# The tail of a fused attention and adapter kernel, put in another order over other PSUM banks

## The chip, the cores and the metric

The kernel runs on one core of a Trainium2 chip. Its time is the device time of one execution, in microseconds (us). The core has five engines that run side by side, each taking its own instructions strictly in order: TensorE (PE; its weight loads are shown apart as PEld), VectorE (DVE), ScalarE (ACT), GpSimd (POOL) and SyncE (SP), which here issues transfers (DMA). They wait for each other through semaphores. TensorE writes only to PSUM, which has eight banks; one bank holds 128 x 512 fp32 numbers.

## The reference, cut to what matters

```python
# attention: q (4, 12288, 128), kv (4, 384, 32, 128)
kv_pool = kv.reshape(B, H // 4, 4, W // 4, 4, C).mean(axis=(2, 4))
k = v = kv_pool.reshape(B, -1, C) @ w_sr             # 768 keys for each batch
a = softmax(q @ k.transpose(0, 2, 1) / np.sqrt(C))
x = (a @ v).reshape(B * S, 128)                      # 49152 tokens
# mixture of adapters: 8 experts of rank 16, the two best for each token
logits = x @ w_gate
w = softmax(the two largest logits)
out = x + sum over the two: w * ((x @ A[e]) @ B[e])
```

## The kernel before

**Tiles.** The 49152 tokens are cut into 96 chunks of 512, numbered c = 0 to 95, 24 for each batch. A chunk is four blocks (NS = 4) of 128 tokens. In the code of the tail, n is 95, the last chunk; n-1, n-2 and so on are those ahead of it.

**What one chunk goes through.** `scores` (line 318) multiplies keys and queries on TensorE, two of six key blocks at a time, into a PSUM tile of two banks, and ScalarE takes the exponential of it into the tile `tt` (line 327). `weigh` (329) makes the weighted sums in two halves of 12 products each: the values carry seven differences of gate logits and a column of ones beside the 128 channels, so one product gives x, its logits and the softmax sum. `normalise` (342), on VectorE, takes reciprocals, multiplies, and finds the largest logits with `max`. `gate` (358) computes the gates' arguments on GpSimd, `gate_tanhs` (378) takes their tanh on ScalarE. `turned("x", ...)` transposes x on TensorE, and a copy takes it to SBUF. `gated_hidden` (437) multiplies the transposed x with A and VectorE multiplies with the gates, which have been spread over rows through memory (`send_gates`, `load_gates`). `up` (481) multiplies with B into a PSUM bank. The output is either `add_rows` (497: VectorE adds x while it reads PSUM), or `take` (489: ScalarE copies PSUM to SBUF) and then `add` (494: GpSimd adds x, since it works on SBUF here), or `x_first` (474: TensorE puts x into the bank with an fp32 identity ahead of `up`) and `take`. `put` (503) sends 256 KB to memory.

**The last six chunks** have no time for the way through memory: their hidden rows are made token by token (`down`, 451, or `hidden`, 803), VectorE multiplies with the gates (`apply_gate`, 463, or `gated`, 778), and TensorE transposes the product (`turn`, 786, or `turned("h", ...)`), which ScalarE copies to SBUF before `up`.

**The order** of all this is written out by hand (`tc.manual_schedule()`): an instruction stands on its engine's queue where the program names it. The waits between engines are put in when the program is built, from which tile each instruction reads and writes; a PSUM tile of two banks counts as one tile there.

**The main loop** (683) runs c from 2 to 94 and weighs chunk c - 1 in pass c. Its last pass, c = 94 = n-1, has extra steps for n-5 and n-4 (695, 718, 740, 744).

**The tail** (749 to 906) gives up the four banks of the scores and makes of them the tiles `e0`, `e1` and `y5`. It weighs n-1 into the banks of `xps` (`y4`) and n into `y5`, with the outputs of n-7 to n-4 between, and finishes the last chunk in two halves: ScalarE writes one, VectorE the other (901 to 905), and the last `put` goes out on ScalarE's queue. `tail_ok` and `all_ok` (570 to 580) count whether the softmax sums were in range; if not, a slow exact path runs, which these inputs do not need.

**Bank names in the tail.** `t_bank()` is the one bank of the transposes, `mtile` the one bank "hd" of the hidden rows and outputs, `fbank(0)` and `fbank(1)` are made from the two banks of `xps` once these are free.

Of the kernel before, what the change touches and what calls it, by code (L numbers as in the profile page):

```python
# [10 lines left out]
FP32 = mybir.dt.float32  # L11
# [5 lines left out]
ALU = mybir.AluOpType  # L17
# [4 lines left out]
def kernel(  # L22
# [175 lines left out]
    def stile(name):  # L198
        return ps_s.tile([P, 2, NTOK], FP32, tag="sg", name=name)
# [251 lines left out]
    def down(c, bank=None):  # L451
        hps[c] = mtile([P, NS, P], name="h_ps") if bank is None else as_tokens(bank)
        for s in range(NS):
            mm(hps[c][:, s], xT[c][:, s], a_bf, start=(s == 0), stop=(s == NS - 1))
# [48 lines left out]
    def put(c, osb, lo=0, hi=NS, queue=None):  # L503
        t0 = c * NTOK
        (queue or nc.sync).dma_start(
            out[t0:t0 + NTOK, :].rearrange("(p s) c -> p s c", p=P)[:, lo:hi], osb[:, lo:hi])
# [16 lines left out]

    def half_out():
        if not spare:
            o = run.tile([P, 2, NS, P], FP32, tag="osb", name="osb", bufs=3)
            spare.extend([o[:, 0], o[:, 1]])
        return spare.pop(0)

    def chunk_ok(c):  # L530
# [37 lines left out]
            nc.vector.tensor_reduce(tot, cnt, axis=AX.X, op=ALU.add)  # L568

    def tail_ok():  # L570
        nc.gpsimd.tensor_scalar(ok[:, tail], rv[:, tail], 1.0 / L_HI, None, op0=ALU.is_ge)
        nc.gpsimd.tensor_scalar(low, rv[:, tail], 1.0 / L_LO, None, op0=ALU.is_le)

    def all_ok(bank):
        n = (NCH - CUT) * NS
        mm(bank[0:1, 0:n], ones_c, ok[:, tail], start=True, stop=False)
        mm(bank[0:1, 0:n], ones_c, low, start=False, stop=True)
        nc.vector.tensor_reduce(last, bank[0:1, 0:n], axis=AX.X, op=ALU.add)
        full = float(P * (NCH * NS + n) + P * 2 * B + 2 * B)
        nc.vector.tensor_scalar(bad, last, tot, full, op0=ALU.add, op1=ALU.not_equal)  # L580

# [98 lines left out]
    for p in range(OWN // 2):  # L680
        sent[2 * p + 3 + (lag(2 * p + 1) > 8)] = p
        fetched[2 * p + 3 + {9: 3 + (lag(2 * p + 3) > 8), 8: 2, 7: 2, 6: 1}[lag(2 * p + 1)]] = p
    for c in range(2, NCH - 1):
        b, k = divmod(c, CPB)
        if c in fetched and lag(2 * fetched[c] + 1) > 8:
            load_gates(fetched[c])
# [31 lines left out]
        if c == NCH - 2:  # L718
            _, evacuate_h = turned("h", c - 4, stile("t_ps")[:, 0])
        next_scores()  # L720
        prep(c)
        k0 = 19 if b == 0 else 17
# [14 lines left out]
            gated_hidden(x)  # L737
        if c in sent:
            send_gates(sent[c])
        if c == NCH - 2:  # L740
            down(c - 3, stile("h_ps")[:, 0])
            apply_gate(c - 3)
        evacuate(c == NCH - 2)
        if c == NCH - 2:
            evacuate_h(True)

    score_banks.close()
    end_banks = ExitStack()  # L750
    ps_e = end_banks.enter_context(tc.tile_pool(
        name="ps_e", bufs=1, reuse_waits="tile", space=bass.MemoryType.PSUM))

    def bank(i):
        return ps_e.tile([P, NTOK], FP32, tag=f"e{i}", name=f"e{i}")

    def gate_args(c, lo, hi, eng, top, arg, msk):
        lg = xn[c][:, lo:hi, C:C + E]
# [59 lines left out]
    def tops4(c, top, y):  # L818
        ri = rinv_all[:, c]
        xv = y[:, :, 0:2 * VW].rearrange("p b (s v) -> p b s v", v=VW)  # L820
        nc.vector.reciprocal(ri.rearrange("p (b s) -> p b s", b=2), xv[:, :, :, VW - 1])
        nc.vector.tensor_tensor(
            xn[c][:, :, 0:C + G].rearrange("p (b s) v -> p b s v", b=2), xv[:, :, :, 0:C + G],
            ri.rearrange("p (b s) -> p b s", b=2).unsqueeze(3).broadcast_to([P, 2, 2, C + G]),
            op=ALU.mult)
        for s in range(NS):
            nc.vector.max(top[:, s], xn[c][:, s, C:C + E])
# [16 lines left out]
    _, evacuate = turned("x", n - 2)
    _, evacuate_h = turned("h", n - 4, bank(0))
    evacuate(True)
    evacuate_h(True)
    up(n - 6, bank(1))
    o6 = take(n - 6)
    h2 = hidden(n - 3, 0, NS, mtile([P, NTOK], name="h2"))  # L850
    up(n - 5, bank(0))
    gate_args(n - 1, 0, NS, nc.gpsimd, top4, arg4, msk4)
    y5 = ps_e.tile([P, 2, 512], FP32, tag="y5", name="y5")
    weigh(n, 0, y5)
    gated(n - 3, 0, NS, gw[q_ - 1][:, 0:NS], h2)
    put(n - 5, add_rows(n - 5))
    add(n - 6, o6, nc.gpsimd)
    put(n - 6, o6)
    turn(high(n - 1), 0, NS, bank(1), xT, n - 1)
    h3 = hidden(n - 2, 0, NS, t_bank())  # L860
    gated(n - 2, 0, NS, gw[q_ - 1][:, NS:2 * NS], h3)
    weigh(n, 1)
    up(n - 4, bank(0))
    gate_tanh(0, NS, arg4)
    o1 = take(n - 4)
    gate_w(0, NS, nc.gpsimd, arg4, msk4)
    tops4(n, top5, y5)
    tail_ok()
    turn(hg[n - 3], 0, NS, mtile([P, NTOK], name="t2"), hgT, n - 3)
    h4 = hidden(n - 1, 0, NS, bank(1))  # L870
    turn(hg[n - 2], 0, NS, t_bank(), hgT, n - 2)
    turn(high(n), 0, NS, bank(0), xT, n)
    gate_args(n, 0, NS, nc.gpsimd, top5, arg5, msk5)
    gate_tanh(0, NS, arg5)
    up(n - 3, mtile([P, NTOK], name="d2"))
    x_first(n - 1, fbank(1), 0, 2)
    gated(n - 1, 0, NS, arg4, h4)
    up(n - 2, fbank(0))
    put(n - 3, add_rows(n - 3))
    put(n - 2, add_rows(n - 2))  # L880
    x3 = ps_e.tile([P, 2, 512], FP32, tag="y5", name="x3")
    h5 = hidden(n, 0, NS, x3[:, 0])
    turn(hg[n - 1], 0, NS, bank(1), hgT, n - 1)
    gate_w(0, NS, nc.gpsimd, arg5, msk5)
    gated(n, 0, NS, arg5, h5)
    x_first(n - 1, fbank(1), 2, 4)
    up(n - 1)
    o4 = take(n - 1)
    put(n - 1, o4)
    add(n - 4, o1, nc.gpsimd)  # L890
    put(n - 4, o1)
    d5 = as_tokens(x3[:, 1])
    for s in range(2):
        mm(d5[:, s], id_f32, xn[n][:, s, 0:C], start=(s == 0), stop=False, skip_group_check=True)
    turn(hg[n], 0, 2, bank(0), hgT, n)
    turn(hg[n], 2, 4, t_bank(), hgT, n, False)
    all_ok(bank(1))
    for s in range(2):
        mm(d5[:, s], hgT[n][:, s], b_bf, start=False, stop=(s == 1), skip_group_check=True)
    o5 = half_out()  # L900
    nc.scalar.activation(o5[:, 0:2], d5[:, 0:2], AF.Copy)
    d6 = as_tokens(mtile([P, NTOK], name="d6"))
    for s in range(2, 4):
        mm(d6[:, s - 2], hgT[n][:, s], b_bf, start=(s == 2), stop=(s == 3), skip_group_check=True)
    nc.vector.tensor_tensor(o5[:, 2:4], d6[:, 0:2], xn[n][:, 2:4, 0:C], op=ALU.add)
# [128 lines left out]
```

## Time and profile before

| what | value |
|---|---|
| median of three runs | 374.78 us (374.4 to 375.65) |
| the profiled execution | 374.92 us |
| its span, first to last instruction | 373.0 us |
| mean granted TensorE clock | 0.999 |
| PE, DVE, ACT, POOL busy | 96%, 80%, 83%, 60% of the span |
| last exponential ends (line 327) | 355.19 us |
| last weighed sum ends (line 338) | 363.42 us |
| last addition ends (line 905) | 369.63 us |

A row of the timeline gives the start in us from the span's beginning, the duration in us, the engine, the line, the operation, the tile written and the tiles read, their sizes and how many instructions were merged into the row; in brackets stands how long the engine had been idle and what released it. A matmul's row reaches to its modelled end; the next matmul starts before that.

### The profile page before, as it was taken

The page shows a single profiled execution, that of the slowest core. Times are in us where ns is not written, and L with a number is a line of the kernel's source. Part 1 is how long each engine was busy: PE and PEld are TensorE (multiplying, and loading weights), DVE is VectorE, ACT ScalarE, POOL GpSimd, SP SyncE. Part 2 cuts the span into 40 slices and gives each one's busy share as a digit, 9 for nine tenths or more (in the row PEclk, how much of TensorE's full clock was granted, in tenths as well). Part 3 has the DMA queues.
Part 4 walks back from the last instruction along what each step waited for, and adds up shares of the span by engine and source line. Part 5 has one row for each costly group of instructions (what it writes and reads, how often), then busy time and mean ns, then how long its engine had stood idle before and what let it go on. Part 6 is the DMA issues. An engine that isn't in the chain of part 4 may idle for free.

```text
span 373.0 us, 10593 instructions
## 1 busy us (share of the span) xinstructions
PE 358.1 (96%) x3945; PEld 263.0 (70%) x3945; DVE 300.2 (80%) x953; ACT 308.7 (83%) x390; POOL 223.5 (60%) x374
## 2 busy tenths in 40 slices
PE   4979999999999999999999999999999999999985
PEld 1446767777777777777777777777777777677774
DVE  3684558888788788888888888888888889988995
ACT  1559999898888888989888988988888889888844
POOL 1003799989699987755679887755624424323244
PEclk9999999999999999999999999999999999999999
DMA  8997999999999999999999999999879899745424
GB/s 260 386 382 177 286 354 291 281 312 330 323 292 311 317 307 258 286 301 317 312 301 338 339 295 313 251 319 246 247 212 253 245 235 241 215 123 132 156 106 181
DMA packets 95594, 101.01 MB, mean 271 GB/s; under 512 B 58804, under 2 KB 59060, under 8 KB 95540
## 3 DMA queue, kind: packets, MB, share of 16 engines
q1 hardware_dynamic: 93924, 99.85, 94.7%
q8 instruction: 31, 0.51, 0.6%
q10 hardware_dynamic: 1616, 0.46, 0.5%
q14 instruction: 23, 0.19, 0.2%
HBM read 62.33 MB, written 25.90 MB: 237 GB/s over the span
## 4 chain that ended last, share of the span: by engine, by line
PE 84%; DMA 7%; DVE 5%; ACT 1%; issue 1%; SPq 1%; POOL 1%; ACTq 0%; DVEq 0%
PE xps L338 34%; PE sg L326 30%; PE t_ps L405 5%; PE d_ps L486 5%; PE h_ps L440 5%; DMA b_f<-in_moe_B_dram 3%; DMA kvt<-in_kv_dram 2%; DMA ge<-g_h 2%; PE v_ps L215 1%; ACT tt L327 1%; DVE xn_all L349 1%; DVE osb L500 1%; DVE ht L443 1%; SPq L87 1%; PE kp_ps L207 0%
## 5 line engine op out<-in xcount | busy, mean ns | idle before, releaser
L327 ACT ACTIVATE tt<-sg 128x1024 f16<-128x1024 f32 x288 | 276.8, 1022 | 37.2 <-PE sg L326 36.5
L326 PE MATMUL sg<-qT,kfT 128*128 128x512 f16 x576 | 170.2, 379 | 0.4 <-ACT qT L593 0.3
L338 PEld LDWEIGHTS <-tt 128*128 128x128 f16 x2304 | 146.1, 98 | 28.3 <-DVE xn_all L349 18.0
L338 PE MATMUL xps<-vext,tt 128*128 128x136 f16 x2256 | 164.7, 223 | 0.3 <-DVE xn_all L349 0.2
L500 DVE TENSOR_TENSOR osb<-d_ps,xn_all 128x512 f32<-128x512 f32 x85 | 58.7, 691 | 28.6 <-PE d_ps L486 27.6
L365 POOL TENSOR_TENSOR arg<-xn_all,top 128x64 f32<-128x64 f32 x47 | 14.4, 306 | 100.0 <-DVE top L356 80.4
L349 DVE TENSOR_TENSOR xn_all<-xps,rinv_all 128x540 f32<-128x540 f32 x94 | 67.7, 720 | 3.2
L326 PEld LDWEIGHTS <-kfT 128*128 128x128 f16 x576 | 49.1, 98 | 24.4 <-issue 1.5
L191 POOL TENSOR_TENSOR kvt<-kvt 128x1024 f32<-128x1024 f32 x27 | 63.7, 2359 | 2.2 <-PE t_ps L405 2.1
L107 POOL CAST q<-q 128x1024 f16<-128x1024 f32 x45 | 46.8, 1040 | 25.1 <-DMA q<-in_q_dram 25.1
L443 DVE SCALAR_TENSOR_TENSOR ht<-ge,h_ps 128x512 bf16<-128x512 f16 x87 | 58.5, 672 | 1.5 <-DMA ge<-g_h 1.1
L486 PEld LDWEIGHTS <-ht 128*128 128x128 bf16 x368 | 26.9, 98 | 24.8 <-DVE ht L443 6.1
L356 DVE MAX8 top<-xn_all 128x8 f32<-128x8 f32 x376 | 35.1, 156 | 6.3
L416 DVE COPY xt<-t_ps 128x512 bf16<-128x512 bf16 x92 | 36.7, 399 | 0.0
L405 PE MATMUL t_ps<-id_bf,xn_all 128*128 128x128 bf16 x376 | 36.3, 219 | 0.0
L486 PE MATMUL d_ps<-b_bf,ht 128*128 128x128 bf16 x340 | 32.9, 219 | 0.7 <-DVE ht L443 0.7
L440 PE MATMUL h_ps<-xt,a_bf 128*128 128x512 bf16 x87 | 33.0, 379 | 0.1
L345 DVE RECIPROCAL rinv_all<-xps 128x4 f32<-128x4 f32 x94 | 17.1, 182 | 13.7 <-PE xps L338 12.2
L405 PEld LDWEIGHTS <-xn_all 128*128 128x128 bf16 x376 | 25.9, 98 | 0.3
L368 POOL TENSOR_SCALAR msk<-msk 128x64 f32<-128x64 f32 x47 | 20.1, 428 | 4.1
L369 POOL TENSOR_TENSOR arg<-arg,msk 128x64 f32<-128x64 f32 x47 | 15.0, 319 | 3.9
L367 POOL TENSOR_TENSOR arg<-arg,msk 128x64 f32<-128x64 f32 x47 | 15.0, 319 | 3.7
(152 smaller groups left out, 221.0 us busy)
## 6 DMA issues: line engine op xcount, KB each, us to landing
kvt<-in_kv_dram SPq DMA_DIRECT2D x48, 512.0 KB
q<-in_q_dram SPq DMA_DIRECT2D x46, 512.0 KB
out_dram<-osb SPq DMA_DIRECT2D x44, 512.0 KB
ge<-g_h SPq DMA_DIRECT2D x45, 256.0 KB
out_dram<-osb SPq DMA_DIRECT2D x7, 256.0 KB
q<-in_q_dram SPq DMA_DIRECT2D x1, 1024.0 KB
qT<-q SPq DMA_TRANSPOSE x46
g_h<-g_sb SPq DMA_DIRECT2D x45, 16.0 KB
```

Source lines behind the costliest of these rows:

```text
L107: nc.gpsimd.tensor_copy(q16[i], q32[i].rearrange("p k n -> p (k n)"))
L191: eng.tensor_tensor(v[:, 0], v[:, 0], v[:, d], op=ALU.add)
L326: mm(sg[:, k], kfT[b][:, j * P:(j + 1) * P], qc, start=True, stop=True)
L327: nc.scalar.activation(tt[c][:, 2 * r:2 * r + 2], sg, AF.Exp, bias=0.0, scale=scale)
L338: mm(o, tt[c][:, j, s * P:(s + 1) * P], vext[b][:, j, 0:VW], start=(j == 0 and s % 2 == 0), stop=(j == NJ - 1 and s % 2 == 1), skip_group_ ...
L349: nc.vector.tensor_tensor(xn[c][:, :, 0:C + G].rearrange("p (b s) v -> p b s v", b=2), xv[:, :, :, 0:C + G], ri.rearrange("p (b s) -> p b ...
L405: mm(columns(t_ps, c, s), src[:, s], id_bf, is_transpose=True, start=(s == 0), stop=(s == NS - 1), skip_group_check=True)
L416: nc.vector.tensor_copy(to, t_ps)
L440: mm(h_ps, a_bf, xT[c], start=True, stop=True)
L443: nc.vector.scalar_tensor_tensor(hgT[c].rearrange("p (k a) t -> p k (a t)", k=2), gE[c // 2][:, h:h + NS // 2].rearrange("p a t k -> p k ( ...
L486: mm(dps[c][:, s], columns(hgT[c], c, s), b_bf, start=(s == 0 and fresh), stop=(s == NS - 1), skip_group_check=True)
L500: nc.vector.tensor_tensor(osb[:, lo:hi], d, xn[c][:, lo:hi, 0:C], op=ALU.add)
```

## The change

The loop ends one pass earlier, and the tail is written anew:

- The steps of pass n-1 are written out. The score banks are given up after the first half of n-2's weighed sums, and become two tiles of two banks each, `z5` and `z4`. n-1 is weighed into `z4`, n into `z5`; both take later products too: `z4` the output of n-5, the hidden rows of n-3 (its second bank), the outputs of n-4, n-1 and half of n; `z5` the hidden rows of n-5 and n, and the transposes of n-2 and n.
- The outputs of n-8, n-7 and n-5 go from VectorE (`add_rows`) to ScalarE and GpSimd (`take`, `add`). That of n-4 went from ScalarE to GpSimd; now TensorE puts its x into the bank and ScalarE takes it.
- `tops4` multiplies the seven logit columns first, takes the maxima, and multiplies the 128 columns of x last: two multiplications for one.
- The half outputs lie in a tile of the pool `kvpool` instead of `osb` pairs.
- `tail_ok` moves from GpSimd to VectorE; the last comparison (`flag`) goes behind the last addition. `all_ok` stands ahead of the last chunk's transposes, and the last addition of n-6 and n-5 on GpSimd stands behind the gates of n.

```diff
     def half_out():
         if not spare:
-            o = run.tile([P, 2, NS, P], FP32, tag="osb", name="osb", bufs=3)
-            spare.extend([o[:, 0], o[:, 1]])
+            o = kvpool.tile([P, 8, NS, P], FP32, tag="kvt", name="osb")
+            spare.extend(o[:, i] for i in range(8))
...
     def tail_ok():
-        nc.gpsimd.tensor_scalar(ok[:, tail], rv[:, tail], 1.0 / L_HI, None, op0=ALU.is_ge)
-        nc.gpsimd.tensor_scalar(low, rv[:, tail], 1.0 / L_LO, None, op0=ALU.is_le)
+        nc.vector.tensor_scalar(ok[:, tail], rv[:, tail], 1.0 / L_HI, None, op0=ALU.is_ge)
+        nc.vector.tensor_scalar(low, rv[:, tail], 1.0 / L_LO, None, op0=ALU.is_le)
...
-    for c in range(2, NCH - 1):
+    for c in range(2, NCH - 2):
...
+        part(C, C + G)
         for s in range(NS):
             nc.vector.max(top[:, s], xn[c][:, s, C:C + E])
+        part(0, C)
...
+    next_scores()
+    weigh(n - 2, 0)
+    z5 = two("b", "z5")
+    z4 = two("a", "z4")
+    down(n - 5, z5[:, 0])
+    apply_gate(n - 5)
+    up(n - 8)
+    o8 = opair[(n - 8) // 2]
+    nc.scalar.activation(o8[:, 1], dps[n - 8], AF.Copy)
+    add(n - 8, o8[:, 1], nc.gpsimd)
...
+    weigh(n - 2, 1)
+    normalise(n - 2)
+    gate(q_ - 1, nc.gpsimd)
+    turned("x", n - 3)[1](True)
+    weigh(n - 1, 0, z4)
+    turn(hg[n - 5], 0, NS, t_bank(), hgT, n - 5)
+    gated_hidden(n - 7)
+    weigh(n - 1, 1)
+    up(n - 7)
+    o7 = take(n - 7)
+    add(n - 7, o7, nc.gpsimd)
+    put(n - 7, o7)
...
+    down(n - 4, fbank(0))
+    tops4(n - 1, top4, z4)
+    gate_args(n - 1, 0, NS, nc.gpsimd, top4, arg4, msk4)
+    apply_gate(n - 4)
+    gated_hidden(n - 6, fbank(1))
+    turned("x", n - 2)[1](True)
+    gate_tanhs(q_ - 1)
+    weigh(n, 0, z5)
+    up(n - 5, z4[:, 0])
+    o5 = take(n - 5)
+    weigh(n, 1)
+    tops4(n, top5, z5)
+    turn(hg[n - 4], 0, NS, t_bank(), hgT, n - 4)
+    h2 = hidden(n - 3, 0, NS, z4[:, 1])
+    h3 = hidden(n - 2, 0, NS, fbank(0))
+    turn(high(n - 1), 0, NS, fbank(1), xT, n - 1)
+    gate_tanh(0, NS, arg4)
+    gate_w(0, NS, nc.gpsimd, arg4, msk4)
+    gate_args(n, 0, NS, nc.gpsimd, top5, arg5, msk5)
+    up(n - 6)
+    gated(n - 3, 0, NS, gw[q_ - 1][:, 0:NS], h2)
+    gated(n - 2, 0, NS, gw[q_ - 1][:, NS:2 * NS], h3)
+    x_first(n - 4, z4[:, 0], 0, 2)
+    turn(high(n), 0, NS, fbank(1), xT, n)
+    h4 = hidden(n - 1, 0, NS, t_bank())
+    gated(n - 1, 0, NS, arg4, h4)
+    x_first(n - 4, z4[:, 0], 2, 4)
     o6 = take(n - 6)
+    turn(hg[n - 3], 0, NS, mtile([P, NTOK], name="t2"), hgT, n - 3)
+    gate_tanh(0, NS, arg5)
+    gate_w(0, NS, nc.gpsimd, arg5, msk5)
+    up(n - 4)
+    h5 = hidden(n, 0, NS, z5[:, 1])
+    turn(hg[n - 2], 0, NS, z5[:, 0], hgT, n - 2)
+    gated(n, 0, NS, arg5, h5)
     tail_ok()
+    up(n - 3, fbank(0))
+    turn(hg[n - 1], 0, NS, fbank(1), hgT, n - 1)
+    o4 = take(n - 4)
+    put(n - 4, o4)
+    for c, o in ((n - 5, o5), (n - 6, o6)):
+        add(c, o, nc.gpsimd)
+        put(c, o)
+    up(n - 2, t_bank())
     put(n - 3, add_rows(n - 3))
+    x_first(n - 1, z4[:, 1], 0, 4)
+    all_ok(mtile([P, NTOK], name="cnt"))
+    turn(hg[n], 0, 2, z5[:, 0], hgT, n)
+    turn(hg[n], 2, 4, z5[:, 1], hgT, n, False)
     put(n - 2, add_rows(n - 2))
     up(n - 1)
+    o1 = take(n - 1)
+    put(n - 1, o1)
+    d5 = as_tokens(z4[:, 0])
     for s in range(2):
         mm(d5[:, s], id_f32, xn[n][:, s, 0:C], start=(s == 0), stop=False, skip_group_check=True)
     for s in range(2):
         mm(d5[:, s], hgT[n][:, s], b_bf, start=False, stop=(s == 1), skip_group_check=True)
+    o0 = half_out()
+    nc.scalar.activation(o0[:, 0:2], d5[:, 0:2], AF.Copy)
+    d6 = as_tokens(fbank(0))
     for s in range(2, 4):
         mm(d6[:, s - 2], hgT[n][:, s], b_bf, start=(s == 2), stop=(s == 3), skip_group_check=True)
+    nc.vector.tensor_tensor(o0[:, 2:4], d6[:, 0:2], xn[n][:, 2:4, 0:C], op=ALU.add)
+    put(n, o0, queue=nc.scalar)
+    flag()
```

More of the change, by code (lines that the diff above doesn't have):

```diff
@@ L739 @@
             send_gates(sent[c])
[L740 to L755, printed above, removed]
+        evacuate()
     def gate_args(c, lo, hi, eng, top, arg, msk):
@@ L842, in fbank @@
         return ps_f.tile([P, NTOK], FP32, tag=f"f{i}", name=f"f{i}")
[L844 to L848, printed above, removed]
-    o6 = take(n - 6)
[L850 to L867, printed above, removed]
-    tail_ok()
-    turn(hg[n - 3], 0, NS, mtile([P, NTOK], name="t2"), hgT, n - 3)
-    h4 = hidden(n - 1, 0, NS, bank(1))
@@ L882 @@
[L882 to L886, printed above, removed]
-    up(n - 1)
[L888 to L892, printed above, removed]
+    up(n - 1)
+    o1 = take(n - 1)
+    put(n - 1, o1)
+    d5 = as_tokens(z4[:, 0])
     for s in range(2):
         mm(d5[:, s], id_f32, xn[n][:, s, 0:C], start=(s == 0), stop=False, skip_group_check=True)
-    turn(hg[n], 0, 2, bank(0), hgT, n)
```

49 lines of the change are left out of this document (17 added, 32 removed).

## The prediction

> **What bounds the kernel now.** The change touches only the last 20 us, so I read the engines' busy time by stretches there first, and then the timeline. The stretches (PE, PEld, DVE, ACT, POOL busy, then clock, share and GB/s of the transfers):
>
> ```profile
> 350.00:355.00 5.00, 5.00 (x64) 3.91 (x62) 4.41 (x17) 4.75 (x6) 2.01 (x6) 1.00 0.49 159
> 355.00:360.00 5.00, 4.38 (x62) 3.57 (x60) 4.93 (x13) 1.53 (x4) 1.85 (x6) 1.00 0.28 108
> 360.00:365.00 5.00, 4.40 (x72) 3.96 (x70) 4.44 (x15) 3.60 (x8) 3.66 (x11) 1.00 0.36 142
> 365.00:373.00 8.00, 3.81 (x44) 3.08 (x41) 3.43 (x8) 2.89 (x7) 2.62 (x7) 0.95 0.48 178
> ```
>
> Up to 355 TensorE is full. From 355 to 360 VectorE is (4.93 of 5 us) while ScalarE, done with the exponentials, works 1.53 us. After 365 nothing is full: there the tail is a chain of hand-offs from engine to engine. The timeline has its main rows, with the starts that give the prices:
>
> ```profile
> 353.25 1.94 ACT L327 ACTIVATE tt<-sg 128x1024 f16<-128x1024 f32 x2
> 353.70 0.87 PE L338 MATMUL xps<-vext,tt 128*128 128x136 f16 x12
> 354.41 0.39 PE L454 MATMUL h_ps<-a_bf,xt 128*128 128x128 bf16 x4
> 357.95 0.68 DVE L466 TENSOR_TENSOR hgs<-h_ps,th 128x512 bf16<-128x512 f32 x1
> 358.55 0.68 DVE L443 SCALAR_TENSOR_TENSOR ht<-ge,h_ps 128x512 bf16<-128x512 f16 x1
> ...
> 360.10 0.39 PE L486 MATMUL e<-b_bf,ht 128*128 128x128 bf16 x4
> 360.32 0.39 PE L806 MATMUL h<-a_bf,xt 128*128 128x128 bf16 x4
> 360.53 0.59 ACT L414 ACTIVATE ht<-e 128x512 bf16<-128x512 bf16 x1
> 361.17 0.38 PE L486 MATMUL e<-b_bf,ht 128*128 128x128 bf16 x4 [0.47 <-ACT ht L414]
> ...
> 362.36 1.27 POOL L495 TENSOR_TENSOR osb<-osb,xn_all 128x512 f32<-128x512 f32 x1
> 362.55 0.87 PE L338 MATMUL y<-vext,tt 128*128 128x136 f16 x12
> 363.46 0.18 DVE L821 RECIPROCAL rinv_all<-y 128x4 f32<-128x4 f32 x1
> 363.68 0.72 DVE L822 TENSOR_TENSOR xn_all<-y,rinv_all 128x540 f32<-128x540 f32 x1
> 363.69 0.60 ACT L491 ACTIVATE osb<-e 128x512 f32<-128x512 f32 x1 [0.44 <-PE e L486]
> 364.18 0.59 ACT L796 ACTIVATE xr<-t 128x512 bf16<-128x512 bf16 x1
> 364.43 0.37 DVE L827 MAX8 top<-xn_all 128x8 f32<-128x8 f32 x4
> 365.06 0.66 PE L478 MATMUL f<-xn_all,id_f 128*128 128x128 f32 x4
> 365.56 0.39 PE L486 MATMUL f<-b_bf,xr 128*128 128x128 bf16 x4
> ...
> 366.68 0.69 DVE L781 TENSOR_TENSOR hgs<-x,r 128x512 bf16<-128x512 f32 x1
> 367.42 0.71 PE L894 MATMUL x<-xn_all,id_f 128*128 128x128 f32 x4
> 367.97 0.27 PE L790 MATMUL e<-id_bf,hgs 128*128 128x128 bf16 x2
> 368.29 0.27 PE L576 MATMUL e<-ok,ones_c 128*1 128x60 f32 x2
> 368.34 0.38 ACT L796 ACTIVATE xr<-e 128x256 bf16<-128x256 bf16 x1
> 368.39 0.27 PE L577 MATMUL e<-low,ones_c 128*1 128x60 f32 x2
> 369.21 0.42 DVE L905 TENSOR_TENSOR osb<-d,xn_all 128x256 f32<-128x256 f32 x1
> 369.72 0.38 ACTq L505 DMA_DIRECT2D out_dram<-osb  x1
> ```
>
> The last weighed sums end at 362.55 + 0.87 = 363.42, the last addition at 369.63: 6.21 us of chain. Then comes the last transfer, issued at 369.72, and the end at 373.0, 3.3 us on.
>
> **Prices read off these rows.** A group of four 128-wide products occupies TensorE for 0.22 us (360.10 to 360.32) and is there after 0.39. Half a chunk's weighed sums occupy it 0.71 (353.70 to 354.41). Two fp32 products with the identity take 0.50 (365.06 to 365.56), so four take 1.0. A count for `all_ok` takes 0.10 (368.29 to 368.39). On ScalarE a 512-wide copy follows another after 0.48 and is there after 0.60; the half copy takes 0.38. A 512-wide VectorE operation follows after 0.60 and is there after 0.68; the last half addition takes 0.42. GpSimd's addition takes 1.27. A hand-off costs 0.05 (360.53 + 0.59 to 361.17).
>
> **The change, part by part.**
>
> *Weighing earlier.* Both kernels agree up to 354.41. From there TensorE's queue is: hidden rows n-5 0.22, output n-8 0.22, second half n-2 0.71, turn n-3 0.22, first half n-1 0.71, to 356.49. The turn of h n-5 needs the transposes' bank, which ScalarE empties 356.02 to 356.62: a stall to 356.67. Then 0.22 for it and 0.22 for `gated_hidden` n-7, whose product goes to VectorE (357.32 to 358.00); second half n-1 ends sooner, so the output of n-7 waits until 358.05. Four groups (0.88), first half n 0.71, output n-5 0.22, second half n 0.71: the last weighed sums are there at 360.74, 2.68 us earlier than 363.42. The scores' banks cost no wait: `z5` needs the last but one exponential (354.2), `z4`, first used near 355.8, the last (353.25 + 1.94 = 355.19).
>
> *Work moved off VectorE.* Three additions less, 3 x 0.60 = 1.8 us. On ScalarE there are three copies more (1.44 us), on GpSimd two additions more net (2.5), on TensorE the x of n-4 (1.0). These queues are in order: what is queued ahead of the last chunk's steps counts.
>
> *The chain from 360.74.* The built program says which tile each instruction waits for; I walk it with the prices above.
>
> 1. VectorE: hand-off 0.05, reciprocal 0.18, logit product 0.19, maxima 0.36, x product 0.62, two hand-offs in between 0.10, gating of n-3 0.68: 362.92. The new logit product (28 columns) has no row. It lies between the reciprocal's 0.18 and the 0.42 of 256 columns; the slope from 256 to 540 columns (0.42 to 0.72) puts it at 0.19, which I take.
> 2. TensorE has done its five groups behind the weighed sums (5 x 0.22) by 361.7 and has the x of n-4 next, for the first bank of `z4`. VectorE is still reading hidden rows n-3 in the second, and the wait is for the tile. So it idles and starts at 362.97; two fp32 products 0.50, turn of x(n) 0.38, hand-off: ScalarE gets it at 363.90.
> 3. ScalarE: copy of x(n) 0.48, then output n-6 0.60: 364.98. The turn of h(n-3) needs the bank "hd" that output n-6 lies in, and stands at the head of TensorE's queue. 0.05 + 0.38 + 0.05: 365.46.
> 4. ScalarE copies h(n-3): 366.06; 0.05, output n-3 0.22, turn of h(n-1) 0.38, 0.05: 366.77. The tanh of n, ready since 364.1, stood behind that copy; with GpSimd's two steps it lets VectorE gate n at 366.85, against 366.68 before. So logits first buys nothing.
> 5. ScalarE: h(n-1) 0.48, output n-4 from `z4` 0.60: 367.85. The x of n-1 goes into the other bank of `z4` and waits for that: 0.05, four fp32 products 1.0, two counts 0.20, first half turn 0.27, 0.05, and 0.02 for reading waits: 369.44. Ahead of them VectorE's moved range tests have over 1 us of cover; were it gone they would cost at most 2 x 0.42.
> 6. ScalarE copies the half: 369.83. The other half's turn goes into the other bank of `z5` and waits: 0.05 + 0.11, output n-1 0.22 + 0.17, 0.05: 370.43. ScalarE takes output n-1: 371.03.
> 7. The last chunk's x goes into the other bank of `z4` and waits for that: 0.05, two fp32 products 0.50, four products of `up` 0.22 + 0.17, 0.05, last half addition 0.42: 372.44.
>
> The same walk over the kernel before ends at 369.58 (trace 369.63). The difference is **+2.86 us**: 2.68 gained on the way to the last weighed sums, 5.5 lost behind them. What follows moves along: outputs n-2 and n-1 are issued about 1.4 and 1.0 us ahead of the last. SP meets GpSimd's late additions (n-6 ready at 369.3), and n-3 queues behind, but that is over before n-2 (371.1). The comparison put behind the last addition (0.2) lies under the transfer, of which 3.3 us follow. The tile from `kvpool` costs nothing, as the last of the 48 row loads there starts at 222.5:
>
> ```profile
> L87 SPq DMA_DIRECT2D kvt<-in_kv_dram x48: 534/579/1717, 0.7 to 222.5; - x48
> ```
>
> Sum: 374.92 + 2.86 = 377.8 for the profiled execution; that one lies 0.14 above the median of 374.78, so **377.7**.
>
> *Bounds.* With fp32 products at 0.28 each (367.42 to 367.97 for two) and the logit product at 0.42 the difference is 3.45; with hand-offs of 0.03, 2.70; with ScalarE's copies following after 0.44, 2.66; fp32 products at 0.20 would give 2.56. The likeliest case's own range is 377.3 to 378.2 (374.78 + 2.56 and + 3.45).
>
> The clock is granted in full until the core falls quiet:
>
> ```profile
> 372.00:372.20 0.20, 0.00 (x0) 0.00 (x0) 0.00 (x0) 0.00 (x0) 0.00 (x0) 1.00 0.00 0
> 372.20:372.40 0.20, 0.00 (x0) 0.00 (x0) 0.00 (x0) 0.00 (x0) 0.00 (x0) 0.68 0.00 0
> 372.40:373.00 0.60, 0.00 (x0) 0.00 (x0) 0.00 (x0) 0.00 (x0) 0.00 (x0) 0.50 0.00 0
> ```
>
> It falls to half some 3 us after the last products (from 368.90). The new tail has pauses of about 1 us at the most, five of them; I count no loss, and the case that they add up is a rival.
>
> **The rivals.**
>
> *The two banks of a tile do not hold each other up* (no change). Steps 2, 5, 6 and 7 each wait for another bank of the same tile. Without these four waits the walk ends at 369.10, 0.48 before the old one: 374.4. For it: no bank is really shared. Against it: the waits stand in the built program. The Trainium skill, page "PSUM — Partial Sum Buffer", section "PSUM bank collisions raise a hardware error", bears on this: engines collide in one bank, not in different banks, and waits by bank would do. By that rule the four waits are not needed, but the program makes them; no row here shows two engines in two banks of one tile.
>
> *The earlier weighed sums carry to the end* (faster). If ScalarE's queue had no more than before ahead of the last chunk's copies, the old 6.21 us would follow 360.74: 366.95 instead of 369.63, so 372.1. For it: VectorE is the full engine from 355 to 360 and loses 1.8 us. Against it: three added copies and an in-order queue. It decides if gating of n starts before 365 rather than at 366.8.
>
> *Some waits are covered.* Without any single one of the four the walk ends at 371.3 to 371.8, so +1.7 to +2.2: 376.5 to 377.0.
>
> *The clock falls in the pauses.* TensorE's share of the chain from 367.9 on is 1.0 + 0.2 + 0.27 + 0.11 + 0.39 + 0.5 + 0.39 = 2.9 us; at half clock that is 2.9 more: 380.6. Against it: 1.00 in the stretch 360 to 365 with 0.6 us idle. The page "TensorE: Matmul & The Clock Gate", section "The HAM clock gate", of the Trainium skill gives about 3.4 us of idleness before the gate closes; the rows above agree (about 3), and by it this rival doesn't happen.
>
> **How the numbers follow.** Forecast 0.80, some waits covered 0.08, clock 0.02: slower, 0.90. Bank-wise waits 0.04: no change. Carried to the end 0.06: faster. About 0.3% (1.1 us) can be told from no change. "Same" gets 0.04, faster 0.06. The range reaches down over the covered waits, 376.5, and up to the bound of 3.45 us and some tenths for hand-offs that no row shows: 376.4 to 378.9.
>
> **What would show it.** Right: the last weighed sums end near 360.7; then idle TensorE ahead of the fp32 products of n-4, n-1 and n, with ScalarE or VectorE as releaser, about 1 us each; gating of n near 366.85; the last addition near 372.4, and 3.4 us from there to the end. Wrong: weighed sums that end after 362, products of `z4` or `z5` that start while the tile's other bank is being read, or a last transfer that lands over 4 us after its issue.

## The result, and the profile after

| | before | after |
|---|---|---|
| median, five runs each | 374.63 us (374.4 to 375.65) | 377.51 us (376.95 to 378.04) |
| ratio, 95% interval | | 1.0072, 1.0051 to 1.0094 |
| profiled execution, its span | 374.92, 373.0 us | 377.46, 375.7 us |
| mean granted clock | 0.999 | 0.998 |
| hidden rows of n-5 start (line 454) | 354.41 us | 353.78 us |
| last weighed sum ends | 363.42 us | 360.13 us |
| last addition ends | 369.63 us | 372.25 us |

The change made the kernel 2.88 us slower by the medians; 377.7 was predicted. The weighed sums are ready earlier, and the end comes later.

The stretches of the kernel after (columns as before: PE, PEld, DVE, ACT, POOL busy, clock, share and GB/s of the transfers):

```profile
355.00:360.00 5.00, 4.92 (x78) 4.41 (x76) 4.49 (x16) 3.14 (x7) 4.37 (x9) 1.00 0.28 108
360.00:365.00 5.00, 3.57 (x51) 3.21 (x49) 3.22 (x10) 2.70 (x7) 2.63 (x11) 1.00 0.14 52
365.00:370.00 5.00, 3.56 (x39) 2.51 (x36) 3.17 (x5) 2.53 (x6) 2.98 (x4) 1.00 0.39 149
370.00:375.70 5.70, 1.11 (x12) 0.75 (x8) 1.42 (x4) 0.98 (x2) 0.00 (x0) 0.88 0.52 199
```

Up to 360 TensorE is full again, where before it waited for VectorE. From 360 to 365 it is busy 3.57 us where the kernel before had 4.40, and no other engine is full: everyone waits. The clock stays at 1.00 to 370 (and on to 374, well past the last product at 371.8), so the pauses cost no clock.

The timeline of the kernel after, with the rows that answer to those of before (here and in the timelines below, rows in between are left out):

```profile
353.78 0.39 PE L454 MATMUL z<-a_bf,xt 128*128 128x128 bf16 x4
...
359.26 0.87 PE L338 MATMUL z<-vext,tt 128*128 128x136 f16 x12
360.17 0.18 DVE L806 RECIPROCAL rinv_all<-z 128x4 f32<-128x4 f32 x1 [0.18 <-PE z L338]
360.39 0.19 DVE L808 TENSOR_TENSOR xn_all<-z,rinv_all 128x28 f32<-128x28 f32 x1
361.49 0.68 DVE L766 TENSOR_TENSOR hgs<-z,th 128x512 bf16<-128x512 f32 x1
362.23 0.71 PE L478 MATMUL z<-xn_all,id_f 128*128 128x128 f32 x4 [0.98 <-DVE hgs L766]
364.33 0.38 PE L775 MATMUL t<-id_bf,hgs 128*128 128x128 bf16 x4 [0.45 <-ACT osb L491]
366.21 0.69 DVE L766 TENSOR_TENSOR hgs<-z,r 128x512 bf16<-128x512 f32 x1 [2.03 <-POOL r L761]
366.56 0.59 ACT L491 ACTIVATE osb<-z 128x512 f32<-128x512 f32 x1
367.20 1.16 PE L478 MATMUL z<-xn_all,id_f 128*128 128x128 f32 x8 [0.68 <-ACT osb L491]
368.72 0.27 PE L577 MATMUL cnt<-low,ones_c 128*1 128x60 f32 x2 [0.17 <-DVE low L572]
369.24 0.38 ACT L781 ACTIVATE xr<-z 128x256 bf16<-128x256 bf16 x1 [2.10 <-PE z L775]
369.68 0.27 PE L775 MATMUL z<-id_bf,hgs 128*128 128x128 bf16 x2 [0.47 <-ACT xr L781]
370.86 0.71 PE L916 MATMUL z<-xn_all,id_f 128*128 128x128 f32 x4 [0.69 <-ACT osb L491]
371.83 0.42 DVE L924 TENSOR_TENSOR osb<-f,xn_all 128x256 f32<-128x256 f32 x1 [0.89 <-PE f L923]
372.33 0.38 ACTq L505 DMA_DIRECT2D out_dram<-osb  x1
```

The reader is to see the brackets: at 362.23, 367.20, 369.68 and 370.86 TensorE stands idle until another engine has done with the *other* bank of `z4` or `z5` (at 362.23 VectorE's gating of n-3, which began at 361.49 and ends at 362.17). The same from the waits, each engine's idle time put down to who ended it (us in total, times, longest):

```profile
PE z L478 <- DVE hgs L766: 1.0, 1, 1.0
PE z L916 <- ACT osb L491: 0.7, 1, 0.7
PE z L478 <- ACT osb L491: 0.7, 1, 0.7
...
PE z L775 <- ACT xr L781: 0.5, 1, 0.5
PE t L775 <- ACT osb L491: 0.5, 1, 0.5
```

**A measure for the tail.** Both programs are the same up to the hidden rows of n-5 (the first row of line 454), but a single execution reaches that point now earlier, now later: in the profiles of this case it lay between 353.29 and 354.41. Most of that arises near the start of the program: after is 0.24 us later than before at the first exponential, 0.76 earlier at the eleventh (31.4 us in before) and 0.63 earlier at the last. So the experiments are compared by two stretches: from that row's start to the issue of the last chunk's output ("tail"), and from there to the end of the span ("rest"). Before they are 15.31 and 3.3 us, after 18.55 and 3.4. Each tail comes from one profile, but the stretch repeats well: from that row to the end of the last weighed sums it takes 6.34 or 6.35 us in after and in all runs but run 5, which changes it.

### The profile page after: what moved, and what is told of

Read it like the earlier page. It is cut to its first block, busy times and chain, and to the rows that moved or that the text cites. A ratio compares the mean times of both kernels' runs of the same rounds, so it can differ in the third digit from the quotient of the medians.

```text
span 375.7 us, 10604 instructions
## 1 busy us (share of the span) xinstructions
PE 358.6 (95%) x3953; PEld 263.7 (70%) x3953; DVE 300.7 (80%) x954; ACT 310.6 (83%) x393; POOL 225.4 (60%) x374
## 4 chain that ended last, share of the span: by engine, by line
PE 87%; DVE 5%; DMA 4%; ACT 1%; issue 1%; ACTq 0%; SPq 0%; POOL 0%; DVEq 0%
PE xps L338 35%; PE sg L326 31%; PE d_ps L486 6%; PE t_ps L405 6%; PE h_ps L440 5%; DMA b_f<-in_moe_B_dram 3%; DMA kvt<-in_kv_dram 2%; PE v_ps L215 1%; DVE kvt L191 1%; DVE xn_all L349 1%; PE z L338 1%; DVE ht L443 1%; PE kp_ps L207 1%; ACT tt L327 1%; DVE osb L500 0%
## 5 line engine op out<-in xcount | busy, mean ns | idle before, releaser
L338 PEld LDWEIGHTS <-tt 128*128 128x128 f16 x2304 | 146.2, 98 | 28.1 <-DVE xn_all L349 17.7
L486 PE MATMUL d_ps<-b_bf,ht 128*128 128x128 bf16 x348 | 33.7, 219 | 0.9 <-DVE ht L443 0.8
```

Source lines behind the costliest of these rows:

```text
L338: mm(o, tt[c][:, j, s * P:(s + 1) * P], vext[b][:, j, 0:VW], start=(j == 0 and s % 2 == 0), stop=(j == NJ - 1 and s % 2 == 1), skip_group_ ...
L486: mm(dps[c][:, s], columns(hgT[c], c, s), b_bf, start=(s == 0 and fresh), stop=(s == NS - 1), skip_group_check=True)
```

## The experiments

The numbers are those of the order in which they ran; the ratio is to the kernel before, on the same chip.

| run | tail | rest | sum | ratio, 95% interval |
|---|---|---|---|---|
| before | 15.31 | 3.3 | 18.6 | |
| after | 18.55 | 3.4 | 21.9 | 1.0072, 1.0051 to 1.0094 |
| 1 single banks, half turn in a free bank | 15.95 | 3.95 | 19.9 | 1.0051, 1.0023 to 1.0080 |
| 2 single banks alone | 16.58 | 4.23 | 20.8 | 1.0047, 1.0031 to 1.0064 |
| 3 range tests earlier | 18.22 | 3.3 | 21.6 | 1.0102, 1.0053 to 1.0150 (two runs, 376.78 and 379.52) |
| 4 the tail in a new order | 13.78 | 5.88 | 19.7 | 1.0015, 1.0001 to 1.0029 |
| 5 outputs back on VectorE | 19.65 | 3.4 | 23.0 | 1.0108, 1.0060 to 1.0155 |
| 6 tanh of n earlier | 18.33 | 3.3 | 21.6 | 1.0070, 1.0040 to 1.0099 |
| 7 half turn alone | 17.92 | 3.3 | 21.2 | 1.0060, 1.0033 to 1.0087 |
| 8 run 1 with the tests of run 3 | 14.73 | 5.85 | 20.6 | 1.0028, 1.0000 to 1.0056 |
| 9 run 4 without two outputs | 13.79 | 3.92 | 17.7 | 0.9955, 0.9933 to 0.9977 |
| 10 run 4, outputs spread | 13.77 | 5.47 | 19.2 | 1.0012, 0.9979 to 1.0046 |
| 11 logits and the rest in one product | 18.48 | 3.3 | 21.8 | 1.0069, 1.0044 to 1.0094 |
| 12 run 10, n-3 ahead of the gates of n | 13.95 | 4.46 | 18.4 | 1.0005, 0.9986 to 1.0025 |

### Do the two banks of one tile hold each other up? (runs 1, 2, 7)

Run 1 gives each bank a tile of its own once n is half weighed, and puts the second half of n's transposes into a bank that is free by then.

```diff
-    z4 = two("a", "z4")
+    z4 = ps_z.tile([P, 2, 512], FP32, tag="a", name="z4")
...
     weigh(n, 0, z5)
-    up(n - 5, z4[:, 0])
+    four.close()
+    up(n - 5, one(0))
...
-    h2 = hidden(n - 3, 0, NS, z4[:, 1])
+    h2 = hidden(n - 3, 0, NS, one(1))
...
-    x_first(n - 1, z4[:, 1], 0, 4)
+    x_first(n - 1, one(1), 0, 4)
...
-    turn(hg[n], 2, 4, z5[:, 1], hgT, n, False)
+    turn(hg[n], 2, 4, fbank(1), hgT, n, False)
```

> All four waits on the other bank of a two-bank tile are taken away: behind n-1's sums z4's two banks become two tiles, and the second half of the last turn goes into fbank(1). The tail, from the hidden rows of n-5 to the issue of the last transfer, is 18.55 us in the changed kernel and 15.31 in the one before. Theory (the waits on the pair's other bank cost the tail): 14.6 us by the walk, up to 15.1 if the range tests still run beside GpSimd's additions; about 374 us. Rival A (the copies moved to ScalarE hold up its queue): those copies are all still there, so at least 17.5. Rival B (the range tests, slowed beside GpSimd's additions, are the loss): at least 18.

Run 2 is the same with the half turn left in `z5`:

> As the run with all four waits gone, but the second half of the last turn stays in the other bank of z5: three of four waits are gone. Theory: a tail of 15.2 to 15.7 us, some 0.6 longer than with all four gone, and an idle TensorE of about 0.5 us ahead of that half turn. Rival A: at least 17.5. Rival B: at least 18.

Run 7 is the half turn alone, all else as changed:

> Only the second half of the last turn is moved from the other bank of z5 to fbank(1): one of the four waits is gone. Theory: the 0.47 us of idle TensorE ahead of that half go, and the tail falls by 0.5 to 0.65, to 17.9 to 18.05 us. If the wait is covered by another, it stays at 18.5.

The tail fell to 15.95 in run 1, 16.58 in run 2 and 17.92 in run 7. So the tiles of two banks cost 18.55 - 16.58 = 1.97 us of tail and the half turn 0.63, and together 2.60, which is their sum. That makes 2.60 of the 3.24 by which the tail of after is longer than that of before, and the rivals' values for runs 1 and 2 (17.5 and more) fall. The time gives back less: tail and rest together fall by 2.0 of 3.3 us in run 1, and its ratio of 1.0051 is not clear of the 1.0072 of after, as the intervals overlap. What the wait was shows in the timeline of run 1:

```profile
360.69 0.66 PE L478 MATMUL o<-xn_all,id_f 128*128 128x128 f32 x4
361.10 0.68 DVE L766 TENSOR_TENSOR hgs<-o,th 128x512 bf16<-128x512 f32 x1
361.32 0.38 PE L775 MATMUL f<-id_bf,xn_all 128*128 128x128 bf16 x4
361.76 0.66 PE L478 MATMUL o<-xn_all,id_f 128*128 128x128 f32 x4
```

The x of n-4 (first row, its second half in the last) starts 7.29 us behind the hidden rows of n-5, where after has 8.45, and VectorE reads the neighbouring bank at the same time (second row, 0.68 us as ever).

The expected sizes of runs 1 and 2 (15.1 and 15.7 at most) were missed by 0.85 and 0.88. Run 1's timeline has the reason:

```profile
364.68 2.48 POOL L495 TENSOR_TENSOR osb<-osb,xn_all 128x512 f32<-128x512 f32 x2
365.36 0.63 DVE L571 TENSOR_SCALAR ok<-rinv_all 128x60 f32<-128x60 f32 x1
365.92 1.30 DVE L572 TENSOR_SCALAR low<-rinv_all 128x60 f32<-128x60 f32 x1
...
367.27 0.27 PE L577 MATMUL cnt<-low,ones_c 128*1 128x60 f32 x2 [0.86 <-DVE low L572]
```

VectorE's two range tests, on 60 numbers a partition, take 0.63 and 1.30 us while GpSimd adds, and TensorE idles 0.86 us for them: the second count starts 1.13 us behind the first, not 0.10 as before. They stood in the way in the kernel after as well, with 0.43 us from one count to the next (0.17 of it idle).

### The range tests beside GpSimd's additions (runs 3, 8)

```diff
     gated(n - 1, 0, NS, arg4, h4)
+    tail_ok()
...
     gated(n, 0, NS, arg5, h5)
-    tail_ok()
```

> The two range tests stand behind the gating of n-1 instead of that of n, at a place where GpSimd waits for the tanh of n; nothing else is changed. Theory: in the changed kernel they took 0.63 and 1.30 us because GpSimd's two additions ran at the same time, and the second count waited for them (0.17 us idle, 0.43 between the counts for 0.10). Here each should take at most 0.3 us, and the tail falls by 0.3 to 0.45, to about 18.1 us. If the operation is slow in itself, they keep 0.6 and 1.3 us. Rival B: the tail falls by 2 us or more.

Run 3's timeline has the tests where GpSimd does nothing:

```profile
363.75 0.18 DVE L571 TENSOR_SCALAR ok<-rinv_all 128x60 f32<-128x60 f32 x1
363.85 0.19 DVE L572 TENSOR_SCALAR low<-rinv_all 128x60 f32<-128x60 f32 x1
...
365.79 2.49 POOL L495 TENSOR_TENSOR osb<-osb,xn_all 128x512 f32<-128x512 f32 x2
```

0.18 and 0.19 against 0.63 and 1.30 for the same instructions, and the tail is 0.33 shorter, just what the counts had lost. (Its two times lie 2.7 us apart, so only the trace is used.) In run 4, where the first test meets an addition and the second doesn't, both prices stand side by side:

```profile
362.82 1.27 POOL L495 TENSOR_TENSOR osb<-osb,xn_all 128x512 f32<-128x512 f32 x1
363.14 1.00 DVE L571 TENSOR_SCALAR ok<-rinv_all 128x60 f32<-128x60 f32 x1
364.05 0.18 DVE L572 TENSOR_SCALAR low<-rinv_all 128x60 f32<-128x60 f32 x1
```

The test that starts inside the addition ends at 364.14, with it (364.09). So it is throughout: of the 26 tests of after and the twelve runs, 14 took 0.22 to 1.31 us, and each of these ended 0.04 to 0.05 us behind the end of an addition; the other 12, which met none or its last 0.04 us, took 0.18 to 0.20. The Trainium skill, page "SBUF — State Buffer", section "SBUF: two separate sides", says that VectorE in a mode that uses both its ports and GpSimd share one pair of ports under an exclusive lock, which the one that starts first holds for its whole instruction. These rows agree, for the case that GpSimd starts first; which mode this instruction runs in they don't show.

Run 8 puts this edit on top of run 1:

> The changed kernel with the first run's single banks and half turn, and VectorE's two range tests moved ahead to just behind the gating of n-1, where GpSimd has no addition. In the first run the tests took 0.63 and 1.30 us beside GpSimd's additions and the second count waited 0.86 us for them; in the run with the tests moved alone they took 0.18 and 0.19 us. Theory (GpSimd's additions hold VectorE's tests up, and the counts with them): the tests take 0.2 us each, the stretch from the start of the hidden rows of n-5 to the issue of the last output falls from 15.95 by 0.5 to 0.9, to 15.0-15.5; from there to the end it stays near 3.9 or grows, as the same outputs have to go out, so the whole gains 0.2-0.8 us on the first run. Rival (the tests only wait beside other work there): the stretch stays at 15.8-16.1.

The tail fell by 1.22 to 14.73, more than expected, and 0.58 below that of the kernel before: the wait for the tests was part of the tail of run 1. Runs 3 and 8 both have the tests out of the way and differ by the four waits alone, by 18.22 - 14.73 = 3.49 us of tail: that is what the waits cost, and the walk had said 372.44 - 369.10 = 3.34. The time didn't visibly follow: the intervals of runs 1 and 8 overlap, and the rest grew from 3.95 to 5.85. In both, the first of the closing outputs (n-4) was issued 12.32 us behind the hidden rows of n-5, and from about 0.9 us later on the transfers hardly paused (287 to 397 GB/s in the full microseconds of run 1, 334 to 412 in those of run 8). That suggests that no longer the chain but the outputs set the end, which runs 9 to 12 take up. In these two profiles the end also came 1.56 and 2.44 us behind the last bytes of the outputs; what that difference is made of stays open.

### The parts that were moved (runs 5, 6, 11)

Run 5 gives the outputs of n-8, n-7 and n-5 back to VectorE.

```diff
-    nc.scalar.activation(o8[:, 1], dps[n - 8], AF.Copy)
-    add(n - 8, o8[:, 1], nc.gpsimd)
+    add_rows(n - 8, osb=o8[:, 1])
...
-    o7 = take(n - 7)
-    add(n - 7, o7, nc.gpsimd)
-    put(n - 7, o7)
+    put(n - 7, add_rows(n - 7))
...
-    o5 = take(n - 5)
+    o5 = add_rows(n - 5)
```

> Outputs n-8, n-7 and n-5 go back to VectorE as one addition each; all else is as in the changed kernel, the two-bank tiles too. Theory: VectorE is again the one that holds up the weighed sums, which end 1 us or more later; the tail grows by about 1.6 us, to 20 us. Rival A (the copies moved to ScalarE are the loss): the tail falls by 1 us or more, to 17.5 or less.

The tail grew by 1.10 to 19.65, less than the 1.6 expected; the weighed sums end 0.91 later (7.26 us behind the hidden rows of n-5 against 6.35), and the second range test took 0.18 us here, so that the counts lost none of their 0.33 us. Moving these outputs off VectorE helps, and isn't what made the kernel slower.

Run 6 moves ScalarE's tanh of n ahead of its copies, and run 11 makes the product of logits and x one instruction again:

```diff
+    gate_tanh(0, NS, arg5)
+    gate_w(0, NS, nc.gpsimd, arg5, msk5)
     o6 = take(n - 6)
```

> The tanh of n goes ahead of output n-6 on ScalarE, so that GpSimd and VectorE can gate n earlier. Theory: gating of n is not on the chain, so the tail stays within 0.3 us of 18.55 (walk: +0.1). A rival by which the late gate of the last chunk sets the end: gating of n starts 1 us or more earlier and the tail falls by as much.

```diff
-        part(C, C + G)
+        part(0, C + G)
         for s in range(NS):
             nc.vector.max(top[:, s], xn[c][:, s, C:C + E])
-        part(0, C)
```

> The changed kernel with the product that normalises n-1 and n made in one piece again, logits and the rest together, as in the kernel before; all else as changed. Theory (as the prediction's fourth step: what starts the gating of n is ScalarE's tanh, behind its copies, so logits first buys nothing): the stretch from the hidden rows of n-5 to the last issue stays at 18.3-18.7 against 18.55. Rival (the logits ahead of the rest carry the gates of n-1 and n): 0.3-0.5 longer, 18.85 or more.

Tails of 18.33 and 18.48 against 18.55: neither the place of the tanh nor the order of the logits matters much. (The 0.22 of run 6 are no gain of the tanh: GpSimd's additions came earlier, the tests took 0.22 and 0.18 us and their 0.33 were saved, so all else grew by 0.11, as in the walk.) In run 6 the gating of n starts 12.50 us behind the hidden rows of n-5, in after 12.43, and another engine releases it:

```profile
365.87 0.60 ACT L781 ACTIVATE xr<-z 128x512 bf16<-128x512 bf16 x1
...
366.57 0.69 DVE L766 TENSOR_TENSOR hgs<-z,r 128x512 bf16<-128x512 f32 x1 [2.11 <-ACT xr L781]
```

The releaser is now ScalarE's copy of h(n-2) out of `z5`, whose other bank holds the hidden rows that VectorE is about to read; it ends at 366.47 (first row). Both engines only read the tile, and even so one waits for the other. So two things were late at the same moment in after, GpSimd's gates and this copy, and taking one away shows the other. In run 10, where these banks are tiles of their own and the tanh stands early as well, the gating of n starts after 11.10 us.

### Can the earlier weighed sums be carried to the end? (runs 4, 9, 10, 12)

Run 4 writes the last steps in another order: single banks, the tests behind the gating of n-1, the gates of n ahead of ScalarE's output n-6, the x of n-1 put in early, n-4's output on VectorE.

```diff
     gated(n - 1, 0, NS, arg4, h4)
+    tail_ok()
+    up(n - 4, one(0))
+    put(n - 4, add_rows(n - 4))
+    x_first(n - 1, b1, 2, 4)
+    turn(hg[n - 3], 0, NS, b3, hgT, n - 3)
+    h5 = hidden(n, 0, NS, one(2))
+    gate_tanh(0, NS, arg5)
+    add(n - 5, o5, nc.gpsimd)
+    put(n - 5, o5)
+    gate_w(0, NS, nc.gpsimd, arg5, msk5)
+    o6 = take(n - 6)
```

> Single banks for all four banks of the sums behind the last weighing, an order made by the walk: the gates' additions behind n-1's arguments on GpSimd, output n-4 by VectorE, x of n-1 and of n put in while TensorE would wait, range tests and counts off the chain. Theory: a tail of 13.7 us, up to 14.4 where tests and additions meet; 1 to 1.6 us below the kernel before, near 373.3 us. Rival A: ScalarE still takes n-8, n-7, n-5 and n-6, so 17 or more.

The tail is as expected, 13.78, and 1.53 below that of the kernel before; the time is not, with a ratio of 1.0015 where 1 to 1.6 us less were expected. The stretches of run 4 near its end:

```profile
366.00:367.00 1.00, 0.89 (x11) 0.42 (x8) 0.83 (x4) 1.00 (x4) 0.00 (x0) 1.00 0.47 172
367.00:368.00 1.00, 0.00 (x0) 0.00 (x0) 0.46 (x2) 0.31 (x2) 0.00 (x0) 1.00 1.06 410
368.00:369.00 1.00, 0.00 (x0) 0.00 (x0) 0.00 (x0) 0.00 (x0) 0.00 (x0) 1.00 1.05 402
369.00:370.00 1.00, 0.00 (x0) 0.00 (x0) 0.00 (x0) 0.00 (x0) 0.00 (x0) 1.00 1.05 408
370.00:371.00 1.00, 0.00 (x0) 0.00 (x0) 0.00 (x0) 0.00 (x0) 0.00 (x0) 0.84 0.91 344
```

All engines are done by 367.5; the DMA engines are full to 370 and nearly so to 371. At 0.262 MB an output, the 1.56 MB of these last four rows are six outputs of 0.65 us each. (The expectation of run 9 says seven; the first of them went out before 367.) Run 9 leaves two of them unwritten:

```diff
     add(n - 5, o5, nc.gpsimd)
-    put(n - 5, o5)
...
     add(n - 6, o6, nc.gpsimd)
-    put(n - 6, o6)
```

> The new tail of the fourth run, with the outputs of chunks n-5 and n-6 computed as before but not written to memory (those two transfers are left out). In the fourth run seven outputs of 0.26 MB went out back to back at some 400 GB/s from 367.0 us, 0.65 us each, and the end came 5.88 us after the last issue. Theory (the closing transfers set the end): the stretch from the hidden rows of n-5 to the last issue stays at 13.6-14.0, the rest falls from 5.88 to 4.6-5.2 (two transfers of 0.65 us, less a gap of up to 0.5 between what is left), sum 18.3-19.1 against 19.66. Rival (the end is a fixed latency after the last issue, or the counts and the flag's test): the rest stays at 5.7-6.0.

The tail stays (13.79), and the rest falls by 1.96, to 3.92: more than the 0.7 to 1.3 expected. In run 4 a thin remainder still ran from 371 to 371.75 (20 GB/s in the microsecond from 371), 4.33 us behind the last issue; in run 9 the last bytes came 2.21 us behind it. The transfers set the end of run 4; the rival (5.7 to 6.0) falls. Run 10 makes the same outputs ready earlier:

```diff
-    tail_ok()
+    put(n - 6, add_rows(n - 6))
     up(n - 4, one(0))
-    put(n - 4, add_rows(n - 4))
...
     put(n - 5, o5)
     gate_w(0, NS, nc.gpsimd, arg5, msk5)
-    o6 = take(n - 6)
+    put(n - 4, add_rows(n - 4))
...
     put(n - 2, add_rows(n - 2))
+    tail_ok()
```

> The new tail of the fourth run, with the outputs ready earlier: VectorE adds n-6 straight from its bank right behind the gating of n-1 (GpSimd's addition and ScalarE's copy of it fall away), the output n-5 is issued ahead of n-4, and the range tests and the counts go behind the last additions. Theory (the closing transfers set the end): the first of the closing outputs is issued near 363.9 instead of 364.86, the stretch to the last issue stays at 13.6-14.0, and the rest falls from 5.88 to 4.9-5.3; the sum is 18.5-19.2 against 19.66, and 18.62 for the kernel before: about the time of the kernel before, 0.3 us to either side. Rival (the outputs of n-1 and n alone set the end): no gain on the fourth run.

The rest fell by 0.41, to 5.47, less than expected. Its stretches show why:

```profile
366.00:367.00 1.00, 0.80 (x10) 0.47 (x10) 1.00 (x3) 0.75 (x4) 0.00 (x0) 1.00 0.99 383
367.00:368.00 1.00, 0.59 (x7) 0.30 (x6) 0.88 (x6) 0.71 (x2) 0.00 (x0) 1.00 0.16 49
368.00:369.00 1.00, 0.00 (x0) 0.00 (x0) 0.10 (x1) 0.00 (x0) 0.00 (x0) 1.00 1.06 410
369.00:370.00 1.00, 0.00 (x0) 0.00 (x0) 0.00 (x0) 0.00 (x0) 0.00 (x0) 0.65 1.06 406
370.00:371.00 1.00, 0.00 (x0) 0.00 (x0) 0.00 (x0) 0.00 (x0) 0.00 (x0) 0.50 0.66 250
371.00:372.00 1.00, 0.00 (x0) 0.00 (x0) 0.00 (x0) 0.00 (x0) 0.00 (x0) 0.50 0.09 31
```

Three outputs now leave early, then the DMA engines have almost nothing for a microsecond (367 to 368), since n-3's output, issued at 366.47, waits for an addition that VectorE makes behind the gating of n. (Its first bytes came near 367.9, later behind the issue than elsewhere; why stays open.) A thin remainder runs on to 371.97 here too. Run 12 swaps the addition and the gating:

```diff
-    gated(n, 0, NS, arg5, h5)
     up(n - 3, fbank(0))
+    put(n - 3, add_rows(n - 3))
+    gated(n, 0, NS, arg5, h5)
...
-    put(n - 3, add_rows(n - 3))
```

> The tenth run's kernel with one swap: VectorE adds n-3 and its output is issued ahead of the gating of n, instead of behind it. In the tenth run VectorE stood idle for 0.33 us before that gating, and the last four outputs, issued from 366.47 on, left a hole in the transfers between 367.0 and 368.0 and then filled 368.0 to 370.6 at some 400 GB/s. Theory (a closing output costs 0.65 us of transfer, and the hole is lost): the gating of n starts about 0.25 us later, the stretch from the hidden rows of n-5 to the last issue grows from 13.77 to 13.9-14.2, the output n-3 fills the hole, and the rest falls from 5.47 to 4.2-4.8; the sum is 18.1-18.9 against 19.24, and 18.62 for the kernel before: between 0.7 us below and 0.2 us above the kernel before, ratio 0.998-1.0005. Rival (the chain, not the transfers, sets the end): the sum stays at 19.1-19.5.

```profile
365.00:366.00 1.00, 0.62 (x8) 0.45 (x8) 1.00 (x4) 0.57 (x3) 0.00 (x0) 1.00 1.03 393
366.00:367.00 1.00, 0.86 (x8) 0.42 (x8) 0.32 (x2) 1.00 (x4) 0.00 (x0) 1.00 0.79 303
367.00:368.00 1.00, 0.00 (x0) 0.00 (x0) 0.48 (x3) 0.13 (x1) 0.00 (x0) 1.00 1.06 406
368.00:369.00 1.00, 0.00 (x0) 0.00 (x0) 0.00 (x0) 0.00 (x0) 0.00 (x0) 1.00 1.06 412
369.00:370.00 1.00, 0.00 (x0) 0.00 (x0) 0.00 (x0) 0.00 (x0) 0.00 (x0) 0.69 0.30 102
```

These stretches of run 12 have no such hole: the tail is 13.95 (0.18 longer), the rest 4.46 (1.01 shorter), both as expected. Not all of the 1.01 is the hole: the last bytes came at 370.26, with less of a remainder than in run 10, and how much of it is chance one profile each can't say. Its median is 374.39 us against 374.70 for the kernel before, the ratio 1.0005 (0.9986 to 1.0025): what the change lost is back, but no version that writes all its outputs is measurably faster than the kernel before. With the chain 1.4 us shorter, the closing outputs have become the bound: run 9 shows it for the order of run 4, and the sum of run 12 lies in its theory's range (18.1 to 18.9) and not in the rival's.

## Why the prediction was right

The predicted walk against the trace of the kernel after, to which 354.41 - 353.78 = 0.63 us is added so that both start at the same point:

| step | predicted | trace + 0.63 |
|---|---|---|
| last weighed sums end | 360.74 | 360.76 |
| 1 gating of n-3 ends | 362.92 | 362.80 |
| 2 x of n-4 starts | 362.97 | 362.86 |
| 3 ScalarE gets the turned h(n-3) | 365.46 | 365.38 |
| 4 gating of n starts | 366.85 | 366.84 |
| 5 output n-4 ends | 367.85 | 367.78 |
| 5 ScalarE gets the half turn of n | 369.44 | 369.87 |
| 7 last addition ends | 372.44 | 372.88 |

- **The forecast (0.80)** held: the weighed sums come 2.7 us earlier and more than that is lost behind them. The new logit product took the 0.19 us that the walk had for it (the slope quoted there gives 0.18).
- **The waits of steps 2, 5, 6 and 7** are there as predicted, with 1.0, 0.7, 0.5 and 0.7 us of idle TensorE, and they are what made the tail longer: runs 1, 2 and 7 take them away and 2.60 of 3.24 us of tail with them, 3.49 by runs 3 and 8. Of the time, run 1 gives back less, since its outputs then follow each other closely to the end; that second bound the prediction did not have.
- **One term was mis-sized: step 5's range tests**, "over 1 us of cover; were it gone they would cost at most 2 x 0.42". They took 0.63 and 1.30 us, 1.85 from the start of the first to the end of the second instead of 0.84, and the second count waited for them. Up to step 5's output n-4 the walk is 0.07 late, behind the counts 0.43 early, and it stays 0.44 early to the end. Of these 0.50, 0.33 are the counts' (run 3); the rest are smaller prices (eight fp32 products 1.09 instead of 1.0, 0.20 instead of 0.10 behind the second count). By runs 3, 4 and 8 the reason is GpSimd's addition beside the tests, which the walk priced as if each engine ran alone.
- That the medians lie 2.88 apart, so close to the +2.86, is in part luck: from the point where the kernels part, after takes 21.9 us and before 18.6, 3.3 more. In the two profiles that point lies 0.63 us apart, and it differs by up to 1.1 from one profile to another, so the difference of two executions is known no better than that. (The sum itself gives 374.78 + 2.86 = 377.64; the 377.7 is rounded twice.)
- **Some waits covered (0.08)** fell: run 7 takes one wait away and the tail falls by 0.63, run 2 the other three and it falls by 1.97.
- **The tanh of n and "logits first buys nothing"** (step 4): right by runs 6 and 11, though the tanh wasn't the only thing that was late.
- **Bank-wise waits (0.04)** fell: the waits are by tile. The rule weighed there, of the Trainium skill's page "PSUM — Partial Sum Buffer", section "PSUM bank collisions raise a hardware error" (a conflict is in one bank, not in different banks), is borne out by run 1: with a tile for each bank TensorE writes one while VectorE reads the next, at 0.66 and 0.68 us.
- **The sums carried to the end (0.06)** fell as a forecast, by its own test: gating of n started at 366.84, not before 365. Run 12 shows that it can be had, but only as far as the outputs allow: the weighed sums' 2.68 us become 1.36 of tail, and none of time.
- **The clock (0.02)** fell: 1.00 throughout the tail, with pauses of up to 0.98 us.

## What to carry to other kernels

In this program a wait goes by the tile, not by what is shared: when a tile of several banks outlives the purpose that needed them together, cut it into tiles of one bank before other engines share it, or an engine will idle for a neighbour that it has nothing to do with. A short VectorE operation between SBUF operands is priced by what GpSimd does beside it (here 0.18 or up to 1.30 us), so put it where GpSimd is idle. At the end of a kernel count the outputs still to go: here 0.65 us each, from some 0.9 us behind the first issue on, and a chain made shorter than that only bunches them.

## What was not expected of the hardware

- VectorE's comparison of 128x60 numbers took 0.18 us alone and 0.63, 1.00 and 1.30 beside GpSimd's additions of 1.27, each time ending 0.04 to 0.05 us behind an addition. VectorE's 512-wide operations with an operand in PSUM kept their 0.68 or 0.69 beside the same additions.
- Outputs of 0.262 MB leave one core at 402 to 412 GB/s when they are queued back to back. The Trainium skill, page "DMA: Bandwidth & Descriptors", section "Where 436 GB/s comes from", gives 435 GB/s for the fabric and some 358 for a core's share of the memory; with one core at work the measurement lies between them.
- From the last bytes of the outputs to the end of the span 13 of the 14 profiles show 1.34 to 1.75 us, run 8 2.44. No run was made to find out what fills it.
- In runs 4 and 10 the last 0.7 to 1.4 us of the transfers were a thin remainder, 20 and 31 GB/s in the microsecond from 371, when most of the bytes had landed. What held it up stays open, and the rests of two single profiles can differ by as much for this alone.
